# Attention, a mixture of experts and a rational feed-forward on one Trainium2 core: how the softmax sums get their constant, two Strassen sums kept in PSUM, shorter GpSimd splits, and a new order table

## The chip, the cores and the metric

One core of one Trainium2 chip runs the whole program: TensorE (PE; its weight loads are PEld), VectorE (DVE), ScalarE (ACT), GpSimd (POOL), and SyncE (SP), which issues nearly all DMAs. The metric is device time in microseconds; lower is better.

## The reference

```
scores = q @ k.T / sqrt(D) + bias(w1, b1, w2)     # B, H, S, D = 2, 8, 576, 64
attn   = exp(scores - max);  attn = attn / (sum(attn) + 1e-9)
x      = attn @ v                                 # as 1152 tokens x 512
for e in range(4):                                # mixture of experts, F = 1024
    out += p[:, e] * (relu(x @ w1[e]) @ w2[e])
h = out @ w_in                                    # second feed-forward, 2048 wide
g = (a0 + a1 h + a2 h^2 + a3 h^3) / (1 + |b0| |h| + |b1| h^2 + 1e-6)
result = g @ w_out
```

All of it is float32. The weights of the last part arrive as 64-bit numbers and are made into float32 on the chip.

## The kernel before

Every float32 product is made of three products of rounded parts: high by high, high by low, low by high. So each operand is split: ACT copies it to the rounded high part, and DVE or POOL subtracts that from the whole to get the low part.

**Attention** (about 62 to 222 us of the span). `attention_setup` describes the work of 8 head pairs n, each of 9 score tiles g: `scores` on PE, `biased` on DVE (adds the bias, finds the maximum), `exps` on ACT (leaves the row sums in `sm`), then on DVE `norm_add` (L610, adds 1e-9 to the sums; two columns for a pair of tiles, one for the ninth) and `norm_recip` (L615), on POOL `norm` (L626, scales a tile of 576 columns). For the ninth tile DVE then repeats its last 64 columns (`repeat`, L619). PE transposes the tiles (`transp`, L643), ACT and DVE split them (`highs`, `lows`, L668 and L672), and PE multiplies with v (`av`, L691). `prepare` splits and transposes the q, k and v of the next head pair (POOL L516, L521; `kl` is k with its halves swapped, by DMA). The class `Flow` is a planner: each operation has a fixed duration and an urgency, the tile number plus an offset out of the table `CFG`, and the planner writes the instructions out in the order that it finds. The engines then run each queue in that order. PSUM gives attention two large buffers (`big`) and four single banks (`one`).

**First stage** (222 to 602 us). Weight pairs p go through `seven(p)`, seven products of Strassen's scheme (`product`, L984, 12 matmuls each) into two PSUM tiles, `y` and `x` (one buffer each, called y and z in `seven`). `keep` copies a product to SBUF; `finish` (L994) adds a later product to that copy, in SBUF, and calls `relu`: ACT writes the high part (L922), and DVE's low part (L923) waits in the list `late` until `flush`. After each product comes one `down` product (L892, six matmuls into one of four banks `ps_o`), which DVE adds to `acc` (L898, L896). `tick` puts one step of a side job ahead of the flush and one behind the down product: first the sums of `sum_steps` (L947 to L956), then the conversion of the 64-bit weights (`conv_f64`: DVE L348, L350, L352, L354). The y tile's next use, the first product of the next pair, needs the low part of the seventh product to be done.

**Weights.** `load_parts` copies the high part on ACT (L289) and makes the low part with one POOL instruction of 128x1024 (L293). `load_differences` makes Strassen's differences on POOL (L320) and their low parts in three pieces, the last of 128x1024 (L317).

**Second stage** (from 602 us). `up()` is one up product (`first`, L1132) with its rational function in three steps that later `up()`s push on; the first steps use PSUM buffers of tag `r` (two), which `x2_T`'s transposes of the accumulated tokens (L1167) use too. Each `up()` also pops one weight load off `loads`, which is set after the last `x2_T`.

Of the kernel before, what the change touches and what calls it, by code (L numbers as in the profile page):

```python
# [24 lines left out]
P = 128  # L25
# [22 lines left out]
OUT_DVE = ()  # L48

LAG = {"PE": .2, "ACT": .16, "DVE": .17, "POOL": .14, "SP": 2.2, "": 0.0, "own": .1, "ownPE": 0.0}  # L50
CFG = dict(S=(-35.26, 125.84, 11.17, 24.1), R=(28.28, -9.74, 22.13, 96.15), E=(77.47, 188.17, -1.12, 46), A=(-77.92, -53.94, -32.86, -44.11), N=(-111.57, 70.25, -249.51, -51.81), T=(34.96, 2.83, 2.3, 19.23), H=(-5.75, 1.88, -115.45, -94.07), L=(-18.35, 27.15, 27.92, 109.33), V=(-121.95, -66.29, -95.72, 89.51), G=(-73.67, -94.88, -129.15, -84.49), X=(-28.43, -204.69, -85.29, -12.23), sk=(45.12, -94.23, 14.39, 29.01), sq=(159.75, 35.05, 115.02, -160.75), sv=(-8.59, 47.12, 159.9, 80.49), qk=(-22.28, -71.03, -0.31, -20.89), qq=(-61.72, 5.89, 4.36, -0.46), kl=(0.11, 48.64, 36.96, 1.84), b=(-48.63, -151.45, 191.1, -105.74), NPB=5, EPS=0.05, w0=30, w1=56, w2=24, rk=(0.98, -24.04, 4.32, 130.75), rq=(-18.89, -50.07, -27.09, -70.45), rv=(-31.38, -71.82, 84.63, 47.31), st=301.74, F=207.64)


class Flow:
# [70 lines left out]
class Kernel:  # L125
# [56 lines left out]
    def setup_const(self):  # L182
        nc, t, c = self.nc, self.t, self.const
        self.identr = c.tile([P, P], F32R, name="identr")
        nc.scalar.activation(out=self.identr, in_=self.ident, func=AF.Copy)

        self.ab = c.tile([P, 8], F32, name="ab")
        nc.sync.dma_start(out=self.ab[:, 0:4], in_=t["moe2_a"].unsqueeze(0).to_broadcast([P, 4]))
        nc.sync.dma_start(out=self.ab[:, 4:6], in_=t["moe2_b"].unsqueeze(0).to_broadcast([P, 2]))
        self.babs = c.tile([P, 2], F32, name="babs")  # L190
        self.one_eps = c.tile([P, 1], F32, name="one_eps")
        nc.vector.memset(self.one_eps, 1.0 + 1e-6)
        self.eps = c.tile([P, 2], F32, name="eps")
        nc.vector.memset(self.eps, 1e-9)
        self.w_max = c.tile([P, 1], F32, name="w_max")
        nc.vector.memset(self.w_max, W_MAX)
        self.dp = c.tile([P, 9, E], F32, name="dp")
        for to, rows in self.token_rows(t["moe_domain_probs"]):
            nc.sync.dma_start(out=self.dp[to], in_=rows)
# [80 lines left out]
    def load_parts(self, i, key, a, b, stg, defer):  # L280
        nc = self.nc
        if key == ("d", 0):
            hi, lo = (self.up.tile([P, a, b], F32R, tag="w64", bufs=2, name="wd" + x) for x in "hl")
        elif len(key) == 2 or (i - 2 * NPAIR + 1) % 10 < 2:
            w = self.wpool.tile([P, 4 * S], F32R, tag="we", bufs=2, name="we")
            hi, lo = (w[:, o:o + a * b].rearrange("p (a b) -> p a b", a=a) for o in (0, a * b))
        else:
            hi, lo = (self.wmoe.tile([P, a, b], F32R, tag="wm" + x, bufs=8, name="wm" + x) for x in "hl")
        nc.scalar.activation(out=hi, in_=stg, func=AF.Copy)  # L289
        self.w_tiles[key] = (hi, lo)  # L290

        def low():
            nc.gpsimd.tensor_tensor(out=lo, in0=stg, in1=hi.bitcast(F32), op=ALU.subtract)  # L293
            self.stage_w()
        defer(low)

    def load_differences(self):


        nc = self.nc  # L300
        key = self.w_plan[self.w_next][0]
        assert key[0] == "u"
        self.w_next += 1
        stg = self.w_staged.pop(0)
        wu = self.w_tiles[key] = self.up.tile([P, 2, 7, 2, P], F32R, tag="wu", bufs=2, name="wu")
        wt = self.up.tile([P, 4, 2, P], F32, tag="wt", bufs=1, name="wt")
        blocks = stg.rearrange("p (x k) (n f) -> p x n k f", x=2, n=2)
        (a, b), (c, d) = ([blocks[:, x, n] for n in range(2)] for x in range(2))
        parts = ((slice(0, 1), blocks[:, 0, 0:1]), (slice(1, 3), blocks[:, 1]), (slice(3, 7), wt))

        def high(i):
            sl, x = parts[i]
            nc.scalar.activation(out=wu[:, 0, sl], in_=x, func=AF.Copy)  # L313

        def low(i):
            sl, x = parts[i]
            nc.gpsimd.tensor_tensor(out=wu[:, 1, sl], in0=x, in1=wu[:, 0, sl].bitcast(F32), op=ALU.subtract)  # L317

        for out, x, y in ((0, b, a), (2, d, b), (1, d, wt[:, 0]), (3, c, wt[:, 1])):
            nc.gpsimd.tensor_tensor(out=wt[:, out], in0=x, in1=y, op=ALU.subtract)  # L320
        yield
        high(0)
        yield
        high(1)
        yield
        high(2)
        for i in range(3):
            low(i)
        self.stage_w()

# [223 lines left out]
    def attention_setup(self):  # L554
# [51 lines left out]

        def norm_add(g):
            n, c, h = where(g)
            sm = sums[n, c][:, 0:h + 1]
            nc.vector.tensor_tensor(out=sm, in0=sm, in1=self.eps[:, 0:h + 1], op=ALU.add)  # L610

        def norm_recip(g):
            n, c, h = where(g)
            ri = rsums[n, c] = early.tile([P, 2], F32, tag="ri", bufs=5, name="ri")
            nc.vector.reciprocal(ri[:, 0:h + 1], sums[n, c][:, 0:h + 1])  # L615

        def repeat(g):
            pt = Pt[g // 9, 4]
            nc.vector.tensor_tensor(out=pt[:, S:S + 64], in0=pt[:, 512:S], in1=pt[:, 512:S], op=ALU.max)  # L619

        def norm(g):
            n, c, h = where(g)
            ri = rsums[n, c][:, h:h + 1]
            pt = Pt[n, c]
            sl = slice(S * h, S * h + S)
            nc.gpsimd.tensor_scalar(out=pt[:, sl], in0=pt[:, sl], scalar1=ri, scalar2=1.0, op0=ALU.mult, op1=ALU.mult)  # L626

        def pt_tiles(n, half):
# [101 lines left out]
        def schedule():  # L730
# [6 lines left out]
            def off(kind, n):  # L737

                return cfg[kind][min(n, 2) + (n == 7)]
# [45 lines left out]
            for n in range(8):  # L785
                p_hold = {}
                for r in range(9):
# [14 lines left out]
                    ao = fl.op("DVE", .11, g + off("A", n), lambda g=g: norm_recip(g), [ao])  # L802
                    for g in ([g] if last else [g - 1, g]):
                        h = (g - 9 * n) % 2
                        no = fl.op("POOL", .72, g + off("N", n), lambda g=g: norm(g), [ao])
                        if last:
                            no = fl.op("DVE", .13, g + off("A", n), lambda g=g: repeat(g), [no])
                        one, one2 = fl.hold("one", 4), fl.hold("one", 4)
                        rest = last or h and c % 2
                        take = [one]  # L810
# [89 lines left out]
    def first_stage(self):  # L900
# [11 lines left out]
        def two(x):  # L912
            return x.rearrange("p (a s) -> p a s", a=2)
# [76 lines left out]
            nc.scalar.activation(out=two(m), in_=ps[:, :, 0:288], func=AF.Copy)  # L990
            return m

        def finish(p, f, b, ps, m):
            nc.vector.tensor_tensor(out=two(m), in0=ps[:, :, 0:288], in1=two(m), op=ALU.add)  # L994
            relu(p, f, b, m, False)

        def seven(p):

# [17 lines left out]
            m5 = keep(z, "m5")  # L1016
            yield
            product(y, p, s3, 5, False, False)
            finish(p, 1, 1, y, m5)
            yield  # L1020
            product(z, p, s4, 2, False, True)
            finish(p, 1, 0, z, u2)
# [33 lines left out]
        for p in range(2, NPAIR):  # L1056
            weights = iter(())
            for i, _ in enumerate(seven(p)):
                tick(i < 6)
                flush()  # L1060
                self.down(p - 1, i)
                tick(i < 6)
                if i == 1:
                    self.load_w()
                    if p < NPAIR - 1:
# [23 lines left out]
    def second_stage(self):  # L1089
# [105 lines left out]
        for t in range(9):  # L1195
# [4 lines left out]
                self.load_w()  # L1200
            if t > 4:
                up()
        x2_T(2, 2)
        loads = [self.load_w] * 6
        for i, (blk, q) in enumerate(units[:-1]):
# [67 lines left out]
```

## Time and profile before

| | us |
|---|---|
| median of 3 runs (lowest to highest) | 816.14 (816.11 to 816.49) |
| the profiled execution | 816.34 |
| its span, first to last instruction | 814.6 |
| busy in the span: PE, DVE, ACT, POOL | 784.9, 675.1, 491.0, 450.1 |

A busy time is a union of an engine's instructions over the whole span, in which stages with different limits follow each other. What matters is therefore what TensorE, the fullest engine, still waits for, and in which stage.

### The profile page before, as it was taken

Reading aid. Unit: us, or ns where it says so; the run is one execution under the profiler, and the core shown is the slowest. Engines: PE = TensorE matmul, PEld = TensorE weight load, DVE = VectorE, ACT = ScalarE, POOL = GpSimd, SP = SyncE. Lnnn points to the kernel's source line nnn. Section 1 sums busy time; section 2 is a strip of 40 time slices with the busy share of each in tenths; the row PEclk is TensorE's granted clock in tenths of the full one; section 3 lists DMA queues with packets and bytes.
Section 4 is the critical chain, followed back from the end, with each engine's and each line's share of the span. In section 5 each row is a group of like instructions: output and inputs, shape, how many; then the busy total and the mean of one; then the engine's idle time right before and its main releaser. Section 6 shows DMA issues by size and latency. Waiting matters only on the chain.

```text
span 814.6 us, 13515 instructions
## 1 busy us (share of the span) xinstructions
PE 784.9 (96%) x4980; PEld 682.6 (84%) x4980; DVE 675.1 (83%) x1160; ACT 491.0 (60%) x932; POOL 450.1 (55%) x398
## 2 busy tenths in 40 slices
PE   5998999999999999999999999999999999999997
PEld 2337898898898988988989998989988899989986
DVE  7987889999688889898888888789668677788775
ACT  5998898999533333333234333323269998877772
POOL 3187688878346554443455444345157977754442
PEclk9999999999999999999999999999999999999999
DMA  5787757571003443443444333433131311000012
GB/s 126 273 297 204 188 155 184 111 185 55 1 28 102 130 130 104 130 122 112 129 130 139 133 109 102 139 128 119 39 104 30 127 53 53 1 0 1 1 39 77
DMA packets 67633, 87.36 MB, mean 107 GB/s; under 512 B 33520, under 2 KB 42096, under 8 KB 67440
## 3 DMA queue, kind: packets, MB, share of 16 engines
q1 hardware_dynamic: 66992, 86.35, 36.0%
q8 instruction: 39, 0.64, 0.3%
q10 hardware_dynamic: 576, 0.16, 0.1%
q14 instruction: 26, 0.21, 0.1%
HBM read 60.12 MB, written 21.36 MB: 100 GB/s over the span
## 4 chain that ended last, share of the span: by engine, by line
PE 72%; DVE 12%; ACT 8%; POOL 2%; DMA 2%; issue 2%; SPq 0%; DVEq 0%; POOLq 0%; ACTq 0%
PE ps_o L892 18%; PE ps_o L1140 11%; PE ps_h L1132 11%; PE ps_y L984 9%; PE ps_x L984 7%; PE ps L691 5%; PE ps L583 4%; PE ps L643 3%; ACT bo L431 2%; ACT hid L402 2%; DVE acc L898 2%; DVE wmag L352 1%; ACT hs L922 1%; PE ps_x L882 1%; DVE wmag L354 1%
## 5 line engine op out<-in xcount | busy, mean ns | idle before, releaser
L892 PE MATMUL ps_o<-we,hs 128*128 128x512 f32 x810 | 203.4, 392 | 0.0
L892 PEld LDWEIGHTS ps_o<-we,hs 128*128 128x128 f32 x810 | 146.1, 188 | 25.8
L293 POOL TENSOR_TENSOR we<-wstg,we 128x1024 fp32r<-128x1024 f32 x20 | 50.1, 2504 | 133.3 <-ACT we L289 133.3
L898 DVE SCALAR_TENSOR_TENSOR acc<-ps_o,prob,acc 128x512 f32<-128x512 f32 x135 | 98.7, 743 | 25.4 <-PE ps_o L892 25.2
L1113 POOL TENSOR_TENSOR qq<-qq,ha 128x384 f32<-128x384 f32 x48 | 49.1, 1023 | 72.3 <-ACT qq L1110 72.3
L1140 PE MATMUL ps_o<-wmh,hs 128*128 128x512 f32 x252 | 83.5, 392 | 0.3 <-POOL hs L1124 0.3
L1132 PE MATMUL ps_h<-x,wmh 128*128 128x384 f32 x288 | 73.6, 336 | 0.0
L626 POOL TENSOR_SCALAR P<-P,ri 128x576 f32<-128x576 f32 x72 | 53.1, 749 | 32.5 <-DVE ri L615 20.5
L922 ACT ACTIVATE hs<-m 128x576 fp32r<-128x576 f32 x28 | 19.2, 687 | 80.3 <-DVE m L994 80.3
L597 DVE CUSTOM_DVE_ANT_0 P<-ps,bias 128x576 f32<-128x576 f32 x72 | 53.4, 750 | 14.4 <-PE ps L583 11.8
L605 ACT ACTIVATE P<-P,nm 128x576 f32<-128x576 f32 x72 | 55.9, 778 | 6.4 <-DVE nm L597 6.0
L413 PE MATMUL ps_ab<-hid,wm 128*32 128x288 f32 x576 | 46.4, 422 | 11.9 <-DVE hid L405 8.2
L1119 DVE SCALAR_TENSOR_TENSOR qq<-qq,rr 128x384 f32<-128x384 f32 x48 | 26.6, 554 | 37.1 <-ACT rr L1118 37.1
L1140 PEld LDWEIGHTS ps_o<-wmh,hs 128*128 128x128 f32 x252 | 47.3, 188 | 10.4 <-POOL hs L1124 1.0
L317 POOL TENSOR_TENSOR wu<-wt,wu 128x1024 fp32r<-128x1024 f32 x14 | 34.6, 2469 | 38.3 <-ACT wu L313 38.3
L1132 PEld LDWEIGHTS ps_h<-x,wmh 128*128 128x128 f32 x288 | 52.5, 188 | 2.0
L583 PE MATMUL ps<-kh,qs 128*128 128x288 f32 x168 | 50.5, 321 | 2.8 <-DVE nm L597 2.7
L984 PEld LDWEIGHTS ps_y<-x,wu 128*128 128x128 f32 x336 | 47.0, 188 | 7.4 <-DVE hs L923 5.7
L984 PE MATMUL ps_y<-x,wu 128*128 128x288 f32 x336 | 49.5, 296 | 3.3 <-DVE hs L923 3.3
L1124 POOL TENSOR_TENSOR hs<-pp,hs 128x384 fp32r<-128x384 f32 x48 | 49.2, 1024 | 3.3 <-issue 2.8
L405 DVE TENSOR_SCALAR hid<-ltab,shift 128x576 f32<-128x576 f32 x108 | 50.3, 537 | 0.0
L672 DVE TENSOR_TENSOR ptl<-ps,pth 128x512 fp32r<-128x512 f32 x72 | 48.4, 682 | 2.2 <-ACT pth L668 1.9
(145 smaller groups left out, 2105.3 us busy)
## 6 DMA issues: line engine op xcount, KB each, us to landing
wstg<-moe_w SPq DMA_DIRECT2D x32, 512.0 KB, 3.7
bias_d<-bo SPq DMA_DIRECT2D x9, 1152.0 KB, 5.3
bias<-bias_d SPq DMA_DIRECT2D x16, 576.0 KB, 5.0
w<-moe_w_in SPq DMA_DIRECT2D x16, 512.0 KB, 4.2
w<-moe_w_out SPq DMA_DIRECT2D x16, 512.0 KB, 3.8
kl<-kh SPq DMA_DIRECT2D x16, 288.0 KB, 4.4
w_u<-wmag SPq DMA_DIRECT2D x16, 256.0 KB, 2.2
w_d<-wmag SPq DMA_DIRECT2D x16, 256.0 KB, 2.4
```

Of the source, the lines that this page charges most:

```text
L293: nc.gpsimd.tensor_tensor(out=lo, in0=stg, in1=hi.bitcast(F32), op=ALU.subtract)
L405: eng.tensor_scalar(out=ht, in0=d, scalar1=c, scalar2=0.0, op0=ALU.add, op1=ALU.max)
L583: nc.tensor.matmul(ps[:, half, dst:dst + w], lhsT=lhs, rhs=k[:, src:src + w], start=(i == 0), stop=(i == len(m) - 1))
L597: nc.vector.tensor_tensor_reduce(out=Pt[u][:, S * h:S * h + S].rearrange("p (a b) -> p a b", a=2), in0=ps[:, :, 0:288], in1=self.bias_t[n ...
L605: nc.scalar.activation(out=pt, in_=pt, func=AF.Exp, scale=-1.0, bias=stat.pop(g), accum_out=sums[n, c][:, h:h + 1])
L626: nc.gpsimd.tensor_scalar(out=pt[:, sl], in0=pt[:, sl], scalar1=ri, scalar2=1.0, op0=ALU.mult, op1=ALU.mult)
L892: nc.tensor.matmul(ps, lhsT=a, rhs=w[:, f, :], start=(f == i == 0), stop=(f == 1 and i == 2))
L898: nc.vector.scalar_tensor_tensor(out=acc[:, t], in0=ps, scalar=pr, in1=acc[:, t], op0=ALU.mult, op1=ALU.add)
L984: nc.tensor.matmul(ps[:, half, 0:288], lhsT=wu[:, w, i, k], rhs=x[v][:, k, 288 * half:288 * half + 288], start=(start and k == j == 0), st ...
L1124: nc.gpsimd.tensor_tensor(out=lo, in0=pp, in1=hi.bitcast(F32), op=ALU.subtract)
L1132: nc.tensor.matmul(ps, lhsT=w[:, k, fo:fo + P], rhs=v[:, k, :], start=(k == i == 0), stop=(k == 3 and i == 2))
L1140: nc.tensor.matmul(ps, lhsT=a[:, P * tt:P * tt + P], rhs=w[:, f % 2, :], start=(f == i == 0), stop=(f == 3 and i == 2))
```

## The change

- `norm_add` adds 1e-9 to one column at a time with a `tensor_scalar`: two instructions for a pair of tiles, one for the ninth. The tile `eps` and its memset are gone.
- `repeat` is gone from DVE. For the ninth tile `norm` has a POOL instruction of 64 columns ahead, which scales the last 64 columns to where the copy stood.
- `load_parts` makes the low part in two POOL instructions of half the size; `load_differences` in four pieces in place of three.
- `finish` writes its sum to PSUM, in place, and the high and low part are read from there. The fifth product of the seven keeps the old way, since its PSUM tile goes on accumulating.
- In the loop over `seven`, the second `tick` of the sixth step (i = 5) moves to the seventh (i = 6).
- In the second stage a fifth `up()` stands ahead of the last tile's transposes; the loads that are popped behind it move one `up()` back.
- The table `CFG` has other numbers, so attention comes out in another order.

```diff
...
+CFG = dict(S=(-46.52, 288.45, 1.92, 183.94), R=(52.57, 7.45, 22.77, 52.37),
...
-            nc.gpsimd.tensor_tensor(out=lo, in0=stg, in1=hi.bitcast(F32), op=ALU.subtract)
+            for k in range(0, a, a // 2):
+                sl = slice(k, k + a // 2)
+                nc.gpsimd.tensor_tensor(out=lo[:, sl], in0=stg[:, sl], in1=hi[:, sl].bitcast(F32), op=ALU.subtract)
...
+        halves = parts[:2] + ((slice(3, 5), wt[:, 0:2]), (slice(5, 7), wt[:, 2:4]))
...
-        for i in range(3):
+        for i in range(4):
             low(i)
...
-            sm = sums[n, c][:, 0:h + 1]
-            nc.vector.tensor_tensor(out=sm, in0=sm, in1=self.eps[:, 0:h + 1], op=ALU.add)
+            for i in range(h + 1):
+                sm = sums[n, c][:, i:i + 1]
+                nc.vector.tensor_scalar(out=sm, in0=sm, scalar1=1e-9, scalar2=None, op0=ALU.add)
...
-        def repeat(g):
-            pt = Pt[g // 9, 4]
-            nc.vector.tensor_tensor(out=pt[:, S:S + 64], in0=pt[:, 512:S], in1=pt[:, 512:S], op=ALU.max)
...
+            if c == 4:
+                nc.gpsimd.tensor_scalar(out=pt[:, S:S + 64], in0=pt[:, 512:S], scalar1=ri, scalar2=1.0, op0=ALU.mult, op1=ALU.mult)
...
-        def finish(p, f, b, ps, m):
-            nc.vector.tensor_tensor(out=two(m), in0=ps[:, :, 0:288], in1=two(m), op=ALU.add)
-            relu(p, f, b, m, False)
+        def finish(p, f, b, ps, m, stays=True):
+
+            c = ps[:, :, 0:288] if stays else two(m)
+            nc.vector.tensor_tensor(out=c, in0=ps[:, :, 0:288], in1=two(m), op=ALU.add)
+            relu(p, f, b, c if stays else m, stays)
...
-            finish(p, 1, 1, y, m5)
+            finish(p, 1, 1, y, m5, False)
...
                 self.down(p - 1, i)
-                tick(i < 6)
+                tick(i != 5)
...
+        up()
         x2_T(2, 2)
```

Three places in the order of the instructions. The first is DVE at the end of one pass over `seven(p)` in the first stage. `ps_x<-ps_x` or `u<-ps_x` is the sum of the sixth product, `hs` are low parts, `wmag` is a step of the weight conversion, `acc` the down products. Before:

```order
L994 TENSOR_TENSOR u_4360<-ps_x,u_4360 128x576
L348 SCALAR_TENSOR_TENSOR wmag<-wmag,w_max 128x512
L923 SCALAR_TENSOR_TENSOR hs<-u_4360,hs 128x576
L898 SCALAR_TENSOR_TENSOR acc<-ps_o,prob,acc 128x512
L350 TENSOR_SCALAR wmag<-wmag 128x512
L923 SCALAR_TENSOR_TENSOR hs<-ps_y,hs 128x576
L898 SCALAR_TENSOR_TENSOR acc<-ps_o,prob,acc 128x512 x3
```

The same stretch of DVE now:

```order
L1004 TENSOR_TENSOR ps_x<-ps_x,u_4402 128x2x288
L359 SCALAR_TENSOR_TENSOR wmag<-wmag,w_max 128x512
L931 SCALAR_TENSOR_TENSOR hs<-ps_x,hs 128x576
L906 SCALAR_TENSOR_TENSOR acc<-ps_o,prob,acc 128x512
L931 SCALAR_TENSOR_TENSOR hs<-ps_y,hs 128x576
L906 SCALAR_TENSOR_TENSOR acc<-ps_o,prob,acc 128x512
L361 TENSOR_SCALAR wmag<-wmag 128x512
L906 SCALAR_TENSOR_TENSOR acc<-ps_o,prob,acc 128x512 x2
```

The second conversion step of the sixth product stood ahead of the low part of y; now it stands behind it and behind one `acc`.

The second place is PE where the second stage begins; `ps_h` are up products, `ps_x` the transposes of the last tile. Before:

```order
L1132 MATMUL ps_h<-x,wmh 128x384 x2
L1132 MATMUL ps_h<-x,wml 128x384
L1167 MATMUL ps_x<-ident,acc 128x128 x4
L1132 MATMUL ps_h<-x,we 128x384 x24
L1132 MATMUL ps_h<-x,wmh 128x384 x2
```

The same stretch of PE now:

```order
L1142 MATMUL ps_h<-x,wmh 128x384 x2
L1142 MATMUL ps_h<-x,wml 128x384
L1142 MATMUL ps_h<-x,we 128x384 x12
L1177 MATMUL ps_x<-ident,acc 128x128 x4
L1142 MATMUL ps_h<-x,we 128x384 x12
```

One up product of 12 matmuls went ahead of the transposes.

The third place is DVE early in attention (head pair 0): `P,nm` is `biased` with its maximum, `ptl` a low part, `sm` the sums, `ri` their reciprocals. Before:

```order
L597 ISA P,nm<-ps,bias 128x576
L597 ISA nm 128x1
L672 TENSOR_TENSOR ptl<-ps,pth 128x4x128
L610 TENSOR_TENSOR sm<-sm,eps 128x2
L597 ISA P,nm<-ps,bias 128x576
L597 ISA nm 128x1
L615 RECIPROCAL ri<-sm 128x2
L672 TENSOR_TENSOR ptl<-ps,pth 128x4x128
```

The same stretch of DVE now:

```order
L608 ISA P,nm<-ps,bias 128x576
L608 ISA nm 128x1
L682 TENSOR_TENSOR ptl<-ps,pth 128x4x128
L608 ISA P,nm<-ps,bias 128x576
L608 ISA nm 128x1
L682 TENSOR_TENSOR ptl<-ps,pth 128x4x128
L622 TENSOR_SCALAR sm<-sm 128x1 x2
L608 ISA P,nm<-ps,bias 128x576
L608 ISA nm 128x1
L627 RECIPROCAL ri<-sm 128x2
```

The addition to the sums stood ahead of a `biased`; now it is two instructions and stands behind that one and behind a low part. PE's own order is the same in this first stretch of attention.

## Rows read from the trace of the kernel before

**Rows 1.** The page, busy time by engine (us, share of the span, instructions).

```profile
PE 784.9 (96%) x4980; PEld 682.6 (84%) x4980; DVE 675.1 (83%) x1160; ACT 491.0 (60%) x932; POOL 450.1 (55%) x398
```

**Rows 2.** Waits of PE: line and tile, releaser, us in total, times, longest.

```profile
PE ps_y L984 <- DVE hs L923: 3.3, 5, 0.7
...
PE ps L583 <- DVE nm L597: 2.7, 4, 1.5
...
PE ps_o L892 <- DVE acc L896: 1.6, 1, 1.6
```

**Rows 3.** The chain that ended last, in order: start us, length us, engine, tile, line.

```profile
281.91 1.58 PE ps_y L984 x12
...
329.87 1.58 PE ps_y L984 x12
...
353.36 1.71 PE ps_y L984 x12
...
568.53 1.58 PE ps_y L984 x12
...
602.70 2.08 PE ps_h L1132 x12
```

**Rows 4.** Timeline, first stage, one pair's end: start us, length us, engine, line, instruction.

```profile
302.44 2.39 POOL L317 TENSOR_TENSOR wu<-wt,wu 128x1024 fp32r<-128x1024 f32 x1 [2.96 <-ACT wu L313]
302.79 2.60 DVE L352 SCALAR_TENSOR_TENSOR wmag<-w,wmag 128x512 uint32<-128x512 uint32 x1
305.31 0.74 DVE L923 SCALAR_TENSOR_TENSOR hs<-ps_y,hs 128x576 fp32r<-128x576 f32 x1
...
306.11 1.06 PE L984 MATMUL ps_y<-x,wu 128*128 128x288 f32 x6 [0.71 <-DVE hs L923]
```

**Rows 5.** Timeline, first stage, the second product's sum and the z tile's next use.

```profile
312.55 0.76 DVE L923 SCALAR_TENSOR_TENSOR hs<-m,hs 128x576 fp32r<-128x576 f32 x1 [0.15 <-ACT hs L922]
...
315.12 1.08 PE L984 MATMUL ps_x<-sums,wu 128*128 128x288 f32 x7
```

**Rows 6.** Groups of instructions, shapes apart: count | busy us, mean ns | idle before.

```profile
L317 POOL TENSOR_TENSOR wu<-wt,wu 128x1024 fp32r<-128x1024 f32 x14 | 34.6, 2469 | 38.3 <-ACT wu L313 38.3
...
L317 POOL TENSOR_TENSOR wu<-wstg,wu 128x512 fp32r<-128x512 f32 x14 | 18.8, 1346 | 16.9 <-ACT wu L313 16.9
...
L610 DVE TENSOR_TENSOR sm<-sm,eps 128x2 f32<-128x2 f32 x32 | 12.5, 392 | 1.2 <-ACT P L605 1.1
...
L610 DVE TENSOR_TENSOR sm<-sm,eps 128x1 f32<-128x1 f32 x8 | 4.9, 611 | 0.0
...
L619 DVE TENSOR_TENSOR P<-P 128x64 f32<-128x64 f32 x8 | 4.4, 549 | 0.1
...
L218 DVE TENSOR_SCALAR ds<-ds 128x9 f32<-128x9 f32 x1 | 0.2, 156 | 0.0
```

**Rows 7.** Timeline ahead of PE's one wait for `acc`, early in the first stage.

```profile
251.15 2.39 POOL L317 TENSOR_TENSOR wu<-wt,wu 128x1024 fp32r<-128x1024 f32 x1
...
252.24 1.91 DVE L956 TENSOR_TENSOR sums<-u,sums 128x576 fp32r<-128x576 f32 x1
```

**Rows 8.** Timeline at the last tile's transposes.

```profile
617.18 0.66 PE L1167 MATMUL ps_x<-ident,acc 128*128 128x128 f32 x4 [0.66 <-DVE x L1170]
...
618.22 0.61 DVE L1121 SCALAR_TENSOR_TENSOR pp<-pp,ab,rr 128x384 f32<-128x384 f32 x1
```

**Rows 9.** Busy time by engine in attention, 62 to 222 us, three stretches summed.

```profile
sum 160.00, PE 152.75 PEld 137.24 DVE 139.27 ACT 135.30 POOL 117.53; mean PE 50.92 PEld 45.75 DVE 46.42 ACT 45.10 POOL 39.18
```

**Rows 10.** Timeline, attention, around PE's longest wait for `biased`.

```profile
67.99 1.41 POOL L521 TENSOR_TENSOR splv<-rawv,splv 128x576 fp32r<-128x576 f32 x1
...
68.27 1.14 DVE L610 TENSOR_TENSOR sm<-sm,eps 128x2 f32<-128x2 f32 x1
...
70.15 0.40 PE L583 MATMUL ps<-kh,qs 128*128 128x288 f32 x1 [1.54 <-DVE nm L597]
```

**Rows 11.** Line L350: count, duration ns min/median/max, first and last start us.

```profile
L350 DVE TENSOR_SCALAR wmag<-wmag x32: 406/849/2510, 264.0 to 572.2; 128x512 uint32<-128x512 uint32 x32
```

More of the change, by code (lines that the diff above doesn't have):

```diff
@@ L50 @@
 LAG = {"PE": .2, "ACT": .16, "DVE": .17, "POOL": .14, "SP": 2.2, "": 0.0, "own": .1, "ownPE": 0.0}
-CFG = dict(S=(-35.26, 125.84, 11.17, 24.1), R=(28.28, -9.74, 22.13, 96.15), E=(77.47, 188.17, -1.12, 46), A=(-77.92, -53.94, -32.86, -44.11), N=(-111.57, 70.25, -249.51, -51.81), T=(34.96, 2.83, 2.3, 19.23), H=(-5.75, 1.88, -115.45, -94.07), L=(-18.35, 27.15, 27.92, 109.33), V=(-121.95, -66.29, -95.72, 89.51), G=(-73.67, -94.88, -129.15, -84.49), X=(-28.43, -204.69, -85.29, -12.23), sk=(45.12, -94.23, 14.39, 29.01), sq=(159.75, 35.05, 115.02, -160.75), sv=(-8.59, 47.12, 159.9, 80.49), qk=(-22.28, -71.03, -0.31, -20.89), qq=(-61.72, 5.89, 4.36, -0.46), kl=(0.11, 48.64, 36.96, 1.84), b=(-48.63, -151.45, 191.1, -105.74), NPB=5, EPS=0.05, w0=30, w1=56, w2=24, rk=(0.98, -24.04, 4.32, 130.75), rq=(-18.89, -50.07, -27.09, -70.45), rv=(-31.38, -71.82, 84.63, 47.31), st=301.74, F=207.64)
+CFG = dict(S=(-46.52, 288.45, 1.92, 183.94), R=(52.57, 7.45, 22.77, 52.37),
+           E=(8.78, 66.35, 136.28, 33.39), A=(54.83, -31.11, -46.06, -28.09),
+           N=(-626.58, -89.98, -9.93, 33.84), T=(113.2, 2.75, 2.45, -168.63),
+           H=(-177.56, -1.07, -82.55, 109.77), L=(-48.72, 27.9, 28.44, 96.87),
+           V=(-146.08, -263.34, -83.98, -64.74), G=(-184.15, 3.42, -48.28, -42.46),
+           X=(-29.7, 7.41, 30.23, 20.21), sk=(-43.56, -73.11, -25.75, -46.52),
+           sq=(-3.51, -291.22, 39.16, 11.06), sv=(-98.75, 28.99, 141.33, 65.56),
+           qk=(121.2, -104.52, -0.3, -80.11), qq=(10.66, -102.36, 4.34, 4.86),
+           kl=(62.79, 21.77, -33.52, -59.48), b=(68.47, -33.03, 128.78, 30.32), NPB=5, EPS=0.05, w0=58,
+           w1=24, w2=56, rk=(-100.56, 26.82, 232.95, -79.05), rq=(22.72, 25.18, 75.42, -71.95),
+           rv=(-58.45, -11.42, 57.85, -75.74), st=1417.27, F=50.61)
 class Flow:
@@ L192, in setup_const @@
         nc.vector.memset(self.one_eps, 1.0 + 1e-6)
-        self.eps = c.tile([P, 2], F32, name="eps")
-        nc.vector.memset(self.eps, 1e-9)
         self.w_max = c.tile([P, 1], F32, name="w_max")
@@ L315, in low @@
         def low(i):
-            sl, x = parts[i]
+            sl, x = halves[i]
             nc.gpsimd.tensor_tensor(out=wu[:, 1, sl], in0=x, in1=wu[:, 0, sl].bitcast(F32), op=ALU.subtract)
@@ L804, in schedule @@
                         h = (g - 9 * n) % 2
-                        no = fl.op("POOL", .72, g + off("N", n), lambda g=g: norm(g), [ao])
-                        if last:
-                            no = fl.op("DVE", .13, g + off("A", n), lambda g=g: repeat(g), [no])
+                        no = fl.op("POOL", .88 if last else .72, g + off("N", n), lambda g=g: norm(g), [ao])
                         one, one2 = fl.hold("one", 4), fl.hold("one", 4)
```

## The prediction

> **What bounds the kernel now.** I began with busy time by engine: TensorE (PE) is busy 96% of the span, the next engine, VectorE (DVE), 83% [rows 1]. So a change can pay only where PE still waits, and the second view is what PE waited for [rows 2]: for the low part of the seventh Strassen product (DVE line L923) 3.3 us in five waits, for attention's `biased` (L597) 2.7 us in four, for an `acc` 1.6 us in one. Behind a wait the trace also shows slower first matmuls, so I took the first stage's loss from the chain instead, by the start of each pair's first product. From 329.87 to 353.36 is a pair with next to no wait: 23.49 us. Twelve pairs lie between 281.91 and 568.53, which is 286.62 us; at 23.49 they would be 281.88. So 4.7 us are lost there [rows 3].
>
> The timeline shows why. At a pair's end DVE has a conversion step, L352, ahead of the low part. L352 starts 0.35 us after a POOL subtraction that takes 2.39 us and lasts 2.60 us itself, to half a microsecond past POOL's end. Only then, at 305.31, does the low part start, and PE's next product sits idle 0.71 us for it [rows 4]. A DVE instruction with its operands in SBUF can so have to wait for a running POOL instruction to end; the same stretch is seen in attention (L610, 1.14 us, to the end of POOL's L521) [rows 10] and on L956 (1.91 us) [rows 7].
>
> **The change part by part.**
>
> *The moved conversion step (first stage): minus 4.7.* The order has the low part of y straight behind an `acc`, with the step behind it. DVE could begin it where L352 began, 302.79 in place of 305.31: 2.5 us earlier, where PE lacked 0.71 [rows 4]. That is more than the wait, so all five go, and I count the whole 4.7 [rows 3]. The step now stands ahead of two `acc`. There are four banks for the down products, so the first `acc` that it delays is wanted by a down product four products later; nobody on PE waits for it sooner. Bounds: 0 and 4.7; I take the whole, since the instruction that made the wait is no longer in front.
>
> *Shorter POOL pieces: minus 1.0.* An instruction of 1024 columns takes 2469 ns, one of 512 takes 1346 [rows 6], so each split adds 0.22 us of POOL time; with 48 more pieces that is 10.7 us on an engine that is busy 55% [rows 1], and its idle time hides it. If POOL were on the path, the 0.22 would show per piece. What it brings is that DVE gets in at half time. The one place where PE paid for that outside the waits above is the 1.6 us for `acc` [rows 2]: L956 stood from 252.24 behind a POOL piece that ran from 251.15 to 253.54 [rows 7]. A first half ends at about 252.5, 1.0 us sooner, and the `acc` behind it moves as much. Bounds 0 and 1.6.
>
> *Sums that stay in PSUM: 0.* The additions and low parts are as many as before. The z tile is now held until its low part is read, not only until its sum is made. In the timeline that low part ends at 313.31 and the z tile's next product starts at 315.12: 1.8 us to spare, which hides it [rows 5]. For what happens without that cover see the third rival.
>
> *The fifth up product: minus 0.4.* Before the last transposes PE sits idle 0.66 us. An up product of 2.08 us [rows 3] in that place would end near 617.18 - 0.66 + 2.08 = 618.6. The transposes then take the other of the two `r` buffers, whose last reader is L1121, done at 618.83 [rows 8]: some 0.2 us of wait stay. Bounds 0 and 0.7. The weight loads that move one product later have a whole block of up products before their use: 0.
>
> *The sums' constant and the dropped copy (attention): minus 2.7.* Off DVE go 12.5 + 4.9 us of L610 and 4.4 of L619, 21.8 in all. On come 2 x 32 + 8 = 72 instructions of one column. No row shows such a one; the nearest is a `tensor_scalar` of 9 columns at 156 ns, so 11.2 us [rows 6]. DVE is 10.6 us lighter in a stretch of 160 where it is busy 139.27 [rows 9]; more to the point, what goes is what stretches to 1.14 us when POOL happens to run [rows 10]. PE's longest wait for `biased`, 1.54 us, follows that stretch directly. I count the 2.7 us of [rows 2]; bounds 0 and 7.25, all of PE's idle time in attention (160.00 - 152.75) [rows 9]. POOL's new instruction of 64 columns, eight times, is 0.36 us by the slope and offset of [rows 6]: 2.9 us on an engine busy 117.53 of 160 [rows 9], hidden.
>
> *The new order table: 0.* It moves nearly everything in attention a few places: `norm`, transposes and the products with v on PE, the splits of the next head on POOL, and on SP the swaps of k (ahead of a bias load at one head) and the first two weight loads (from the middle of attention to behind the last bias loads). PE's order is the same in head pair 0 and keeps its pattern later. No row prices it. A gain is capped by the 7.25 above; a loss by nothing, and I take 3 us, about what the four waits cost now, for the range.
>
> The sum is 4.7 + 1.0 + 0.4 + 2.7 = 8.8 us, off the profiled execution's 816.34 (span 814.6 and 1.7 around it, which stay): **807.5 us**. The median of the runs is 0.2 below that execution, which I leave.
>
> **The rivals.**
>
> *First, the single columns wait as the pairs did, and the kernel gets slower.* L610 and L619 read two tensors from SBUF, the new instruction one. For it: L350, also a `tensor_scalar` on SBUF with one tensor input, takes 406 ns at best but 849 in the median and 2510 at most [rows 11], so one input does not save an instruction from waiting. Against: that one has 512 columns, and no row shows a one-column instruction beside a POOL one. [...] The price: without L610 and L619 DVE has 117.5 us in attention [rows 9]. At 0.61 us a column, what the one-column L610 took [rows 6], 72 add 44: 161.5 in a stretch of 160. Were DVE then as full as PE is now (95%), attention would take 169, 9 more, and with the 6.1 off for the other parts the time is 819. DVE begins to set the time at 0.49 us a column (95% of 160), and from 0.57 on the loss is more than the 6.1. If they wait only a little, attention gives nothing and the time is 810.
>
> *Second, the new order eats the gain.* DVE, ACT and PE are all above 84% in attention [rows 9], so a few exchanged places can leave PE behind a late `biased` or a late swap of k. With the 2.7 gone and up to 3 lost: 810 to 813.
>
> *Third, a new wait for the z tile.* Between sum and low part DVE has a conversion step; if it stood behind a POOL piece by more than the 1.8 us of [rows 5], PE would wait. The pieces are at most 1.35 us now [rows 6], so it needs a queue behind one. In five of twelve pairs at 0.7 us, as the old wait: 3.5 back, 811.
>
> *Fourth, the moved step does not free y.* If something else on DVE holds the low part back as long, the 4.7 stay: 812.2.
>
> **How the numbers follow.** The forecast has 0.68, the second rival 0.14, the first 0.09 (0.05 of it slower, 0.04 near 810), the third 0.04, the fourth 0.05. The likeliest gives 807.5. The low end takes the upper bounds: 4.7 + 1.6 + 0.7 and 6.3 of attention's 7.25, 803.0. The high end keeps the 4.7 alone and lets attention lose 1: 812.5, which takes in most of the second and third rivals and the fourth. What is left out is the slower case, the second rival's far end, and a gain beyond the counted waits. About 0.2%, 1.6 us, is what a measurement of this kernel can tell from no change. Faster by more than that: 0.88. Within: 0.07, from the second rival's far end (0.04) and mild cases of the first and fourth (0.03). Slower: 0.05.
>
> **What would show it.** In the trace after: PE's waits for the low part (`ps_y` behind `hs`) gone, and pairs of 23.5 us all through; the wait for `acc` near 0.6; the last transposes with a wait of 0.2; no one-column addition above 0.2 us, and DVE some 10 us lighter in attention; PE's idle time there near 4.5 us. It is wrong if the columns are stretched beside POOL, if attention's stretch is not shorter by 2 to 3 us, or if PE shows a wait for `ps_x` in the first stage.

## The result and the profile after

The changed kernel takes 808.14 us (median of 4, 807.95 to 808.74) against 816.26 (816.11 to 816.49): a ratio of 0.990, 95% interval 0.988 to 0.992. Its profiled execution took 807.95 us, with a span of 806.0 beside 814.6.

The table has the stages by the starts of PE's matmuls at their borders (first scores, the first stage's first up product, first and last Strassen product, the second stage's first up product, first and last product of the last stage), from the two traces.

| Stage, us | before | after | difference | predicted |
|---|---|---|---|---|
| bias, up to the first scores | 58.95 | 59.75 | +0.80 | 0 |
| attention | 162.91 | 158.51 | −4.40 | −2.7 |
| block of sums, up to the first Strassen product | 36.40 | 35.45 | −0.95 | −1.0 |
| first stage's Strassen products | 329.35 | 324.58 | −4.77 | −4.7 |
| rest of the down products | 14.84 | 14.96 | +0.12 | 0 |
| up products and last transposes | 21.47 | 21.11 | −0.36 | −0.4 |
| last stage | 185.78 | 186.74 | +0.96 | 0 |
| its end | 4.86 | 4.85 | −0.01 | 0 |
| span | 814.56 | 805.95 | −8.61 | −8.8 |

The sum came out as forecast, but attention and the last stage did not, and the bias phase is longer. The page's row of busy times, answering [rows 1]:

```profile
PE 783.1 (97%) x4980; PEld 683.0 (85%) x4980; DVE 649.4 (81%) x1183; ACT 488.3 (61%) x932; POOL 455.0 (56%) x454
```

What PE waited for (line and tile, releaser, us in total, times, longest), answering [rows 2]:

```profile
PE ps L594 <- DVE nm L608: 1.3, 4, 0.5
PE ps_o L1150 <- POOL hs L1134: 1.1, 2, 0.9
PE ps_o L900 <- DVE acc L904: 0.6, 1, 0.6
PE ps L653 <- ACT qs L556: 0.5, 1, 0.5
PE ps_x L1177 <- DVE pp L1131: 0.2, 1, 0.2
```

The wait for the low part (`ps_y` behind `hs`) has no row any more, `acc` stands at 0.6 and the last transposes at 0.2. New is the second row: in the last stage PE waits for POOL. The chain, answering [rows 3], has pairs of 23.49 us (273.25 to 296.74) all through:

```profile
273.25 4.10 PE ps_o L900 x18
...
296.74 4.10 PE ps_o L900 x18
```

Why the low part is early, in the timeline at the end of a pair, answering [rows 4]: L931 now starts half a microsecond after the POOL piece does, and the conversion step (L363, two places later) takes 1.27 us in place of 2.60.

```profile
297.97 2.54 POOL L328 TENSOR_TENSOR wu<-wt,wu 128x512 fp32r<-128x512 f32 x2 [2.94 <-ACT wu L324]
...
298.47 0.76 DVE L931 SCALAR_TENSOR_TENSOR hs<-ps_y,hs 128x576 fp32r<-128x576 f32 x1
...
299.81 1.27 DVE L363 SCALAR_TENSOR_TENSOR wmag<-w,wmag 128x512 uint32<-128x512 uint32 x1
```

In the window of [rows 9] (62 to 222 us) PE is idle 4.31 us in place of 7.25 and DVE 9.7 us lighter. The window now holds 3.7 us of the next stage; from border to border of attention PE is idle 4.32 in place of 7.44, and DVE goes from 140.4 to 127.7. The 72 one-column additions (count, shortest, median and longest in ns) never stretch, though a POOL instruction is running at the start of 47 of them:

```profile
sum 160.00, PE 155.69 PEld 141.01 DVE 129.60 ACT 134.60 POOL 121.17; mean PE 51.90 PEld 47.00 DVE 43.20 ACT 44.87 POOL 40.39
```

```profile
L622 DVE TENSOR_SCALAR sm<-sm x72: 133/144/156, 63.1 to 205.9; 128x1 f32<-128x1 f32 x72
```

### The profile page after: what moved, and what is told of

It reads as the page before. It is cut to its first block, busy times and chain, and to the rows that moved or that the text cites. A ratio compares the mean times of both kernels' runs of the same rounds, so it can differ in the third digit from the quotient of the medians.

```text
span 806.0 us, 13644 instructions
## 1 busy us (share of the span) xinstructions
PE 783.1 (97%) x4980; PEld 683.0 (85%) x4980; DVE 649.4 (81%) x1183; ACT 488.3 (61%) x932; POOL 455.0 (56%) x454
## 4 chain that ended last, share of the span: by engine, by line
PE 77%; ACT 7%; POOL 6%; issue 4%; DVE 4%; DMA 2%; SPq 0%; POOLq 0%; DVEq 0%; ACTq 0%
PE ps_o L900 20%; PE ps_o L1150 11%; PE ps_y L992 10%; PE ps_h L1142 10%; PE ps_x L992 8%; PE ps L701 6%; PE ps L594 5%; PE ps L653 4%; ACT hid L413 2%; ACT bo L442 2%; POOL we L303 2%; PE ps_x L890 1%; PE ps L548 1%; POOL wml L303 1%; PE ps_y L890 1%
## 5 line engine op out<-in xcount | busy, mean ns | idle before, releaser
L303 POOL TENSOR_TENSOR we<-wstg,we 128x512 fp32r<-128x512 f32 x40 | 57.0, 1446 | 130.3 <-ACT we L297 130.3
L1123 POOL TENSOR_TENSOR qq<-qq,ha 128x384 f32<-128x384 f32 x48 | 48.9, 1019 | 71.0 <-ACT qq L1120 71.0
L930 ACT ACTIVATE hs<-ps_x 128x576 fp32r<-128x576 f32 x32 | 20.8, 651 | 80.7 <-DVE ps_x L1004 74.0
L328 POOL TENSOR_TENSOR wu<-wt,wu 128x512 fp32r<-128x512 f32 x28 | 36.2, 1314 | 36.4 <-ACT wu L324 36.4
L416 DVE TENSOR_SCALAR hid<-ltab,shift 128x576 f32<-128x576 f32 x108 | 52.6, 558 | 0.0
L1134 POOL TENSOR_TENSOR hs<-pp,hs 128x384 fp32r<-128x384 f32 x48 | 48.9, 1019 | 3.5 <-issue 2.8
L424 PEld LDWEIGHTS ps_ab<-hid,wm 128*32 128x32 f32 x576 | 18.4, 112 | 37.0 <-ACT bo L442 13.9
L1150 PE MATMUL ps_o<-wml,hs 128*128 128x512 f32 x126 | 49.5, 393 | 0.0
```

The source lines that it names most:

```text
L303: nc.gpsimd.tensor_tensor(out=lo[:, sl], in0=stg[:, sl], in1=hi[:, sl].bitcast(F32), op=ALU.subtract)
L416: eng.tensor_scalar(out=ht, in0=d, scalar1=c, scalar2=0.0, op0=ALU.add, op1=ALU.max)
L424: nc.tensor.matmul(ps[32 * q:32 * q + 32, i, 0:288], lhsT=wm, rhs=hs[q][:, 288 * i:288 * i + 288], start=True, stop=True)
L1150: nc.tensor.matmul(ps, lhsT=a[:, P * tt:P * tt + P], rhs=w[:, f % 2, :], start=(f == i == 0), stop=(f == 3 and i == 2))
```

## The experiments

Each runs beside the kernel before on the same chip; its median is in the text. The stage lengths are read from the traces as in the table above, since they tell more than the medians: those of the kernel before alone go from 816.26 to 817.85. One thing has to be known for that: in six of the fourteen profiled executions PE's granted clock is at 0.50 over 66 to 68 us (0.57 in e1) in place of 1.00 (the last section has the rows). Attention is then some 1.0 to 1.5 us longer: 159.55, 159.58 and 159.96 in three kernels whose attention is that of the changed one, against 158.48 to 158.54 in three others without the fall. "With the fall" marks such a run below.

### First stage: which of the two edits frees y?

**The step back in its old place** (e1).

```diff
-                tick(i != 5)
+                tick(i < 6)
```

> The conversion step goes back to where it stood, ahead of the fifth product's low part; POOL's subtractions stay in halves. Theory A (the place made the wait, as the prediction says): PE waits for the low part of the seventh product again in several pairs, 12 pairs lose up to 4.7 us, about 812.8 us. Theory B (the length of POOL's piece made it): a piece is at most 1.45 us in place of 2.5, so the step ends about 1.1 us sooner than before, more than the 0.71 us that PE lacked; no such wait comes back and the time stays at 808.1.

Measured: 807.47 us, first stage 324.61, no wait for the low part. Theory B. The trace at the same pair's end shows how: the step stands ahead of the seventh product's low part again (the expectation calls it the fifth's), but ends behind POOL's first half, after 1.50 us, and the low part starts 1.77 us after POOL's start.

```profile
299.11 3.00 POOL L328 TENSOR_TENSOR wu<-wt,wu 128x512 fp32r<-128x512 f32 x2 [2.94 <-ACT wu L324]
...
299.45 1.50 DVE L363 SCALAR_TENSOR_TENSOR wmag<-w,wmag 128x512 uint32<-128x512 uint32 x1
...
300.88 0.74 DVE L931 SCALAR_TENSOR_TENSOR hs<-ps_y,hs 128x576 fp32r<-128x576 f32 x1
```

**POOL's pieces whole again** (e2), the step still moved.

```diff
-            for k in range(0, a, a // 2):
-                sl = slice(k, k + a // 2)
-                nc.gpsimd.tensor_tensor(out=lo[:, sl], in0=stg[:, sl], in1=hi[:, sl].bitcast(F32), op=ALU.subtract)
+            nc.gpsimd.tensor_tensor(out=lo, in0=stg, in1=hi.bitcast(F32), op=ALU.subtract)
...
-            sl, x = halves[i]
+            sl, x = parts[i]
...
-        for i in range(4):
+        for i in range(3):
```

> POOL's low parts in the pieces of before (one of 1024 columns, three of 1, 2 and 4 blocks); the step stays moved. Theory A (place): the wait for the seventh product's low part stays away; the wait for acc in the block of sums is 1.6 us again (+1.0), and the second stage gets back the 1.0 us that it lost where PE waited for POOL: near 808.1. Theory B (length): waits for the low part come back, 2 to 4.7 us more, 810 to 813.

Measured: 808.77 us; first stage 324.58, no wait for the low part: theory A here. The block of sums is 36.64 (+1.19, the wait for `acc` 1.8) and the last stage 185.69 (−1.05, the wait for POOL 0.3):

```profile
PE ps_o L897 <- DVE acc L901: 1.8, 1, 1.8
...
PE ps_o L1147 <- POOL hs L1131: 0.3, 1, 0.3
```

**Both undone** (e9: the edits of e1 and e2 together).

> Both undone: step ahead of the low part and POOL in whole pieces, the rest as in the changed kernel (sums in PSUM, columns, table, fifth product). If place and length are the whole cause of the first stage's loss, all five waits and their 4.7 us come back: 812.8 less the 1.0 of the second stage plus the 1.0 of the acc, about 812.8. If the sums in PSUM take part (their additions and low parts have an operand outside SBUF), less comes back, about 810.

Measured: 812.55 us; first stage 328.85, and the five waits are back, as for place and length as the whole cause:

```profile
PE ps_y L989 <- DVE hs L928: 2.8, 5, 0.7
```

At the pair's end POOL, the step and the low part are those of [rows 4] again, the low part 2.87 us after POOL's start:

```profile
298.17 2.40 POOL L325 TENSOR_TENSOR wu<-wt,wu 128x1024 fp32r<-128x1024 f32 x1 [2.94 <-ACT wu L321]
...
298.51 2.60 DVE L360 SCALAR_TENSOR_TENSOR wmag<-w,wmag 128x512 uint32<-128x512 uint32 x1
...
301.04 0.74 DVE L928 SCALAR_TENSOR_TENSOR hs<-ps_y,hs 128x576 fp32r<-128x576 f32 x1
...
301.84 0.40 PE L989 MATMUL ps_y<-x,wu 128*128 128x288 f32 x1 [0.65 <-DVE hs L928]
```

So either edit alone gives the whole 4.3, and the second adds nothing. The kernel before is 0.5 longer still, but e11 below, whose first stage has the code of before, is at 328.87: in the four kernels that have the five waits (before, e9, e10, e11) they cost 4.3 to 4.8 us. The move takes 2.6 us out of the way of y; the halves take 1.1 us (2.87 less 1.77), and PE lacked only 0.7. What mattered is the shortfall, not the size of the obstacle.

**The sums in SBUF again** (e3).

```diff
-            c = ps[:, :, 0:288] if stays else two(m)
+            c = two(m)
...
-            relu(p, f, b, c if stays else m, stays)
+            relu(p, f, b, m, False)
```

> The two sums go back to SBUF. Theory A (they are worth nothing, as the prediction says): 808.1, no new wait of PE in the first stage. Rival (an addition and a low part with all operands in SBUF but one wait for POOL where those on PSUM do not): additions and low parts of the two products are stretched by up to a POOL piece, 1.4 us, and PE waits in some pairs: 809 to 811.

Measured: 808.07 us (with the fall), first stage 324.58 to the hundredth, no new wait: theory A. The sums in PSUM are worth nothing here, since neither product's low part was late.

### Last stage: where the 0.96 us went

**Halves for the first stage's weights only** (e8).

```diff
-            for k in range(0, a, a // 2):
-                sl = slice(k, k + a // 2)
+            n = a // 2 if len(key) == 2 else a
+            for k in range(0, a, n):
+                sl = slice(k, k + n)
```

> POOL's low part of 1024 columns is halved only for the first stage's weights; the second stage's go back to one piece. Theory A (the second stage's 0.96 us of loss are the two halves, 0.22 us longer together than the whole, on a POOL that PE waits for): second stage 185.7 us in place of 186.74, the block of sums stays at 35.45 and the first stage at 324.6, so 1.0 us less than the changed kernel: 807.1. Rival (it is the fifth up product, which moves a weight load): second stage stays at 186.7, 808.1.

Measured: 807.56 us (with the fall), last stage 185.67, block of sums 35.45, first stage 324.58: theory A. The timelines of POOL and PE at the same place, first of the changed kernel:

```profile
629.12 1.01 POOL L1134 TENSOR_TENSOR hs<-pp,hs 128x384 fp32r<-128x384 f32 x1
...
630.10 1.01 POOL L1123 TENSOR_TENSOR qq<-qq,ha 128x384 f32<-128x384 f32 x1
...
631.07 2.54 POOL L303 TENSOR_TENSOR wml<-wstg,wmh 128x512 fp32r<-128x512 f32 x2
...
633.57 1.01 POOL L1134 TENSOR_TENSOR hs<-pp,hs 128x384 fp32r<-128x384 f32 x1
...
634.63 0.50 PE L1150 MATMUL ps_o<-wmh,hs 128*128 128x512 f32 x1 [0.90 <-POOL hs L1134]
```

and of this run:

```profile
629.16 1.03 POOL L1135 TENSOR_TENSOR hs<-pp,hs 128x384 fp32r<-128x384 f32 x1
...
630.13 1.03 POOL L1124 TENSOR_TENSOR qq<-qq,ha 128x384 f32<-128x384 f32 x1
...
631.11 2.43 POOL L304 TENSOR_TENSOR wml<-wstg,wmh 128x1024 fp32r<-128x1024 f32 x1
...
633.47 1.04 POOL L1135 TENSOR_TENSOR hs<-pp,hs 128x384 fp32r<-128x384 f32 x1
...
634.55 0.50 PE L1151 MATMUL ps_o<-wmh,hs 128*128 128x512 f32 x1 [0.28 <-POOL hs L1135]
```

POOL has no idle time here: each up product brings it one L1134, one L1123 and one weight's low part, and they follow each other without a gap from 616.70 to 645. A round from one L1134 to the next is 4.45 us with two halves and 4.31 with the whole piece. The sixth L1134 of the stage (28.10 us after the stage's first product against 27.18) is 0.92 us late, and PE pays that. Over the kernel POOL is 56% busy; over this stretch it is the bound.

**Without the fifth up product** (e4).

```diff
-        up()
         x2_T(2, 2)
```

> The fifth up product ahead of the last tile's transposes is taken out. Theory A (as predicted, it is worth 0.4): the stretch from the first up product to the first product of the last stage is 21.1 us plus 0.4 less what the second stage changes; second stage still 186.7, so 808.5. Rival (it moves the weight load and so makes the second stage's loss): second stage 185.8 and the sum of both 0.6 shorter, 807.5.

Measured: 808.11 us; up products and transposes 21.49 (+0.38), last stage 186.55. Theory A: the product is worth 0.38 of the 0.4 predicted, and has no part in the 0.96. The transposes wait 0.6 us again where the changed kernel waits 0.2:

```profile
PE ps_x L1177 <- DVE x L1180: 0.6, 1, 0.6
```

### Attention: columns, copy and table

**The old table in the changed kernel** (e5).

```diff
-CFG = dict(S=(-46.52, 288.45, 1.92, 183.94), R=(52.57, 7.45, 22.77, 52.37),
+CFG = dict(S=(-35.26, 125.84, 11.17, 24.1), R=(28.28, -9.74, 22.13, 96.15), E=(77.47, 188.17, -1.12, 46),
...
```

> The changed kernel with the order table of before. Attention was 162.91 us before and is 158.51. Theory A (table nothing, columns and dropped copy all 4.4): attention stays at 158.5, 808.1. Theory B (columns and copy give the 2.7 predicted and the table the rest, by the swap of k ahead of a bias load, whose 1.24 us of waiting for a transfer at 94 us are gone): attention about 160.2, 809.8. Theory C (the table is the whole gain): attention 162.9, 812.5.

Measured: 811.64 us, attention 161.33. Between theories B and C: going back to the old table costs the changed kernel 2.82, and columns and copy together have 1.58 left. PE's busy time from 100 to 180 us is 79.10 of 80 here, 79.87 in the changed kernel.

**The columns alone in the kernel before** (e10).

```diff
-            sm = sums[n, c][:, 0:h + 1]
-            nc.vector.tensor_tensor(out=sm, in0=sm, in1=self.eps[:, 0:h + 1], op=ALU.add)
+            for i in range(h + 1):
+                sm = sums[n, c][:, i:i + 1]
+                nc.vector.tensor_scalar(out=sm, in0=sm, scalar1=1e-9, scalar2=None, op0=ALU.add)
```

> The kernel before, with nothing changed but the sums' constant (one column at a time, one tensor on input); the order of all else stays. Theory A (what PE waited behind the two-input additions, 2.7 us by the prediction): attention 162.9 less 2.7, 160.2, and 813.6 in all. Theory B (by the run with the pairs back, which cost attention 1.8 us once the lower clock of its one stretch is taken off): 161.1, 814.5. Rival (in this order other waits take their place, the table was needed): 162.9, 816.3.

Measured: 816.21 us against 817.85, a ratio of 0.998 (0.997 to 0.9995); attention 161.24, 1.67 less: theory B to 0.14. PE's order in attention is that of the kernel before throughout. PE's waits for `biased` fall from 2.7 us to 1.6, the longest from 1.5 to 0.6; of the other three, 0.3 to 0.6 each before, all are at 0.3 now:

```profile
PE ps L583 <- DVE nm L597: 1.6, 4, 0.6
```

That is 1.1 of the 1.67. The rest comes from a wait that the prediction did not count: before, PE waited 1.2 us at 95 us for the swap of k (first line); here that is gone, and 0.5 for `norm` at 91 us is new (second line). Why the swap is in time here was not tried.

```profile
PE ps L583 <- DMA kl<-kh: 1.2, 1, 1.2
```

```profile
PE ps L644 <- POOL P L627: 0.5, 1, 0.5
```

**The table alone in the kernel before** (e11; the table's lines of the diff, nothing else).

> The kernel before, with nothing changed but the order table. Theory A (the table is worth its 2.8 us by itself, as it was to the changed kernel): attention 160.1, 813.5. Theory B (it is fitted to the changed instructions and worth little without them): 162 to 164, 815 to 817.

Measured: 823.64 us, a ratio of 1.007 (1.005 to 1.010): slower. Attention is 170.11 (with the fall), 7.2 longer, and some 6 once the fall is taken off; neither theory gave so much. Two waits make up most of what the trace names, but in the kernel before they stood at 2.7 and 1.2, so they have grown by 1.4 only:

```profile
PE ps L593 <- DVE nm L607: 3.6, 8, 0.7
...
PE ps L593 <- DMA kl<-kh: 1.7, 1, 1.7
```

So the two are not to be added. With the old table the dropped copy is worth nothing beyond the columns (161.33 with both, 161.24 with the columns alone); with the copy and the pairs in place the new table loses some 6; with both edits it gains 2.8.

These figures price more than a table. The change also alters what the planner `Flow` is given: `repeat` is no longer one of its operations, and the ninth tile's `norm` has a longer duration.

```diff
-                        no = fl.op("POOL", .72, g + off("N", n), lambda g=g: norm(g), [ao])
-                        if last:
-                            no = fl.op("DVE", .13, g + off("A", n), lambda g=g: repeat(g), [no])
+                        no = fl.op("POOL", .88 if last else .72, g + off("N", n), lambda g=g: norm(g), [ao])
```

From one table and the other list of operations it makes a third order: in e11 PE's order parts from that of both kernels at 84 us, in e5 from the changed kernel's at 109 us and from that of before at 138. The next two runs have the pairs, but no copy, and PE's order is the changed kernel's throughout. Attention in the first of them is 8.75 shorter than in e11, both with the fall, and the edits outside attention do not move it (e1 to e4, e8, e9). So it is not the pairs that cost so much in e11, but what comes with the copy: the copy itself or the order that is planned with it. Which of the two was not tried.

**Pairs with two inputs** (e6), in the changed kernel.

```diff
-            for i in range(h + 1):
-                sm = sums[n, c][:, i:i + 1]
-                nc.vector.tensor_scalar(out=sm, in0=sm, scalar1=1e-9, scalar2=None, op0=ALU.add)
+            sm = sums[n, c][:, 0:h + 1]
+            nc.vector.tensor_tensor(out=sm, in0=sm, in1=self.eps[:, 0:h + 1], op=ALU.add)
```

> The sums get their constant from a second tile again, two columns at a time (tensor_tensor), as before; table, dropped copy and the rest stay changed. Theory A (a two-input instruction on SBUF waits for POOL, and biased behind it): single ones reach 0.6 to 1.4 us, PE's waits for biased come back, 2 to 3.4 us of them, attention 160.5 to 162, 810 to 811.5. Rival (the table has moved them off POOL's pieces, or the dropped copy was the gain): attention 158.5, 808.1.

**Pairs with one input** (e7).

```diff
-            for i in range(h + 1):
-                sm = sums[n, c][:, i:i + 1]
-                nc.vector.tensor_scalar(out=sm, in0=sm, scalar1=1e-9, scalar2=None, op0=ALU.add)
+            sm = sums[n, c][:, 0:h + 1]
+            nc.vector.tensor_scalar(out=sm, in0=sm, scalar1=1e-9, scalar2=None, op0=ALU.add)
```

> The changed kernel, with the constant added to both columns at once by a tensor_scalar: one tensor on input as in the changed kernel, two columns as in the kernel before. Theory A (a second input from SBUF is what makes an addition wait for POOL): none above 0.2 us, attention 158.5, 808.1. Theory B (more than one column is): single ones reach 1.4 us as in the run with pairs and two inputs, attention 160.3, 809.9.

Measured: 810.31 us with two inputs and 808.93 with one; attention 161.36 and 160.65, both with the fall. Against the three kernels with the fall and the changed attention (159.55 to 159.96) that is 1.4 to 1.8 and 0.7 to 1.1 us. The additions (two inputs, then one):

```profile
L623 DVE TENSOR_TENSOR sm<-sm,eps x40: 140/366/1380, 64.0 to 208.6; 128x2 f32<-128x2 f32 x32, 128x1 f32<-128x1 f32 x8
```

```profile
L621 DVE TENSOR_SCALAR sm<-sm x40: 127/169/1403, 64.2 to 208.1; 128x2 f32<-128x2 f32 x32, 128x1 f32<-128x1 f32 x8
```

For e6 theory A holds on the instructions (to 1.38 us); in size it comes out just under its range (159.9 to 160.3 of attention once the fall is taken off), and PE's waits for `biased` are only 1.5 us, where the changed kernel has 1.3, so the loss is not in them. For e7 theory B holds on the instructions, while the time lies between A and B: with one input, 19 of the 32 pairs take over 200 ns, the longest 1403, while its eight one-column ones stay at 127 to 144. With two inputs the one-column ones stretch too, 6 of 8, to 843 ns. That they wait for POOL shows in their ends: all 19 had a POOL instruction running at their start and end 21 to 25 ns after it does, while the nine pairs that started beside none took 157 to 169. In e6 the 26 stretched ones end 3 to 20 ns after POOL's. In the changed kernel 41 of the 47 single columns that start beside POOL end before its instruction does, by up to 1.0 us. Of the four forms run here only one column with one input never stretches (156 ns at most).

### A version that is faster than both

In the changed kernel PE waits 2.2 us at the start of attention for an eviction of the bias phase that stands behind an exp on ACT. The last run takes e8 and moves the last of these evictions to DVE, ahead of the second `biased` (e12).

```diff
-OUT_DVE = ()
+OUT_DVE = (35,)
...
-            if gg:
+            if 0 < gg < NG:
                 combine(gg - 1)
+            if gg == NG - 1:
+                combine(gg)
```

> The version with the halves in the first stage only, and one more edit at the start of attention: of the bias phase's 36 groups the last one's eviction (bo) goes from ACT, where it stands behind an exp, to DVE, ahead of the second biased. Theory A (PE's 2.2 us there is that eviction: it ended at 64.71 in the changed kernel, the one before it at 62.88): PE's transposes of k start near 62.9 in place of 64.76, attention is 1.9 us shorter, 157.6 at the full clock (156.6 to 157.6), and where the half clock of some runs near 66 to 69 us followed that idle stretch it may go too, another 1.0; 805 to 806 in all. Rival (k's late evictions or the last bias load, which moves one place back on SP, are next): attention as before, 158.5 to 159.6, 807 to 807.6.

Measured: 806.63 us (805.54 to 806.93), a ratio of 0.988 (0.986 to 0.989) to the kernel before, the fastest median here. Against the changed kernel that is 1.5 us, and the two ratios' intervals overlap; in the traces the last stage, which e8's edit shortens, gives 1.0 (185.73 against 186.74). The transposes start at 62.25 without a wait, yet attention is 158.65: the rival. PE gives the 2.2 us back within ten, in new waits for POOL's `norm` and for `biased`:

```profile
PE ps L597 <- DVE nm L611: 2.2, 3, 1.6
PE ps L656 <- POOL P L639: 1.1, 1, 1.1
```

What this run gains over e8 is the absence of the fall in its profile; its four timed runs have mean granted clocks of 0.999 to 1.000, where three of the four of e8 have 0.997. Four runs don't show that the edit is the reason.

## Why the prediction was right, point by point

That the sum is within 0.6 us of the measured time is luck in part. Attention gave 1.7 us more than forecast, and the last stage and the bias phase took 0.96 and 0.80 that were not forecast; the three nearly cancel. By its own sign (attention shorter by 2 to 3 us, where it is 4.4) the attention part was wrong.

**The moved step, −4.7: −4.77.** Size and view were right: the loss read from the pairs' pace, not from the 3.3 us of waits (other kernels with the five waits lose 4.3 to 4.7). The slower first matmuls are in the trace of the kernel before: 397 to 399 ns behind each of the five waits, 292 to 295 in eight of the other nine pairs (402 in the ninth, which had no wait). The reason was half of it. I gave the shorter pieces no share in these waits, and e1 shows that they remove all five by themselves; with e9 the pair of edits is the cause, and either is enough.

**Shorter pieces, −1.0: −0.95 in the block of sums.** The `acc` wait went from 1.6 to 0.6 as worked out, and e2 brings it back (+1.19). **But their cost, 0, was wrong: +0.96.** The step that failed is "its idle time hides it", drawn from POOL's 55% over the whole span. I wrote that the 0.22 would show per piece if POOL were on the path and did not look for a stretch where it is. It is one at the start of the last stage: e8 takes the pieces out there and gets the 0.96 back. Per round the price was 0.14, not 0.22.

**Sums in PSUM, 0: 0** (e3). **Fifth up product, −0.4: −0.36** (e4: 0.38), with the 0.2 us wait that was foreseen.

**Columns and copy, −2.7: −1.6 to −1.7** (e5, e10). The step that failed is counting all four waits for `biased` as made by L610. In e10 1.1 of the 2.7 us went, 0.9 of it from the longest, the one whose cause [rows 10] show. And a wait that I had not counted went with them, that for the swap of k. The duration was well bounded: 145 ns mean where I took 156 from nine columns, so 10.4 us for the 72 where I had 11.2.

**The table, 0: −2.8, together with the dropped copy and the order planned without it.** I gave it no gain because no row priced it. It more than hid the miss of the columns: 1.6 + 2.8 = 4.4, where 2.7 + 0 stood. The range's low end, with 6.3 us from attention, covers it.

**The first rival** (single columns wait for POOL as well) is refuted: 156 ns at most in 72. In e7 the pairs reach 1403 ns and the single columns 144; why one column is spared no run shows. **The second rival** (the new order eats the gain) came out the other way in the changed kernel and is real without the other edits, by some 6 us (e11). **The third and fourth** did not happen: no wait for `ps_x` in the first stage, none for y.

**Bias phase, +0.80,** at which no edit of the change is aimed. Its length lies between 58.95 and 59.86 us over all fourteen profiled executions; kernels in which the code of this phase is that of before have 58.95, 59.62 and 59.86. I take it for scatter; what sets it was not tried.

## What to carry to other kernels

A share of busy time over the span doesn't say that an engine has room: before you lengthen its work, look for the stretch where its instructions follow each other without a gap. Ask of a wait by how much the late one is late, since any edit that wins that much removes it and a second one adds nothing. A planner's table belongs to the operations that it was made for: with the old ones it gave another order and lost some 6 us of attention, with the new ones it gained 2.8.

## What the runs showed of the hardware

**Which DVE instructions wait for POOL.** The 72 one-column `tensor_scalar` with one SBUF input took 133 to 156 ns in the changed kernel (the 47 that start beside a running POOL instruction 133 to 155) and 131 to 156 in e10, with a median of 144 in both: none stretched. Two columns take up to 1.4 us (1403 ns in e7), one column with two SBUF inputs up to 1.2 (1246 ns in the kernel before, where the six of eight that start beside POOL take 420 or more). I had expected either the width or the second input to matter; either was enough.

**The clock at the start of attention.** The stretches from 62 us on in the changed kernel and in e8 (window, its length, PE busy and instructions, granted clock, DMA share, GB/s):

```profile
62.00:64.00 2.00, 0.59 (x6) 1.00 0.33 118
64.00:66.00 2.00, 1.24 (x11) 1.00 0.63 134
66.00:68.00 2.00, 2.00 (x16) 1.00 0.85 293
68.00:70.00 2.00, 1.52 (x13) 1.00 0.91 165
```

```profile
62.00:64.00 2.00, 0.23 (x4) 1.00 0.13 43
64.00:66.00 2.00, 1.60 (x14) 0.99 0.82 203
66.00:68.00 2.00, 2.00 (x11) 0.50 0.82 255
68.00:70.00 2.00, 2.00 (x13) 0.66 0.97 189
70.00:72.00 2.00, 1.33 (x11) 1.00 1.10 233
```

After PE had been busy 0.23 us of 62 to 64, the granted clock in e8 is 0.50 over 66 to 68, 0.66 over 68 to 70 and 1.00 from 70 on; the changed kernel, busy 0.59 us of the same stretch, kept 1.00. Of fourteen profiled executions six fell (e1, e3, e6, e7, e8, e11). Idle time there is not enough to bring it: the kernel before had PE busy 0.02 us of 62 to 64, e9 0.00, and both kept 1.00. What brings it no run shows. Attention is 1.0 to 1.5 us longer with it (159.55 to 159.96 against 158.48 to 158.54), as much as the smaller edits of this change.
